# A pair's fourth step and its tail as one step of three rows, and last keys' transposes moved to VectorE, in a top-k attention with a low-rank mixer

## Chip, core and metric

One core of one Trainium2 chip runs the whole kernel. The metric is the device time in microseconds of one execution. The kernel before takes 1706.43 us (median of 3 runs, 1706.23 to 1707.57).

## The reference

Two blocks follow each other, all in float32 on 8 batches, 8 heads, 576 positions, head size 64:

```python
# attention, each batch and head
scores = q @ k.T / 8
kth = 32nd largest of each row of scores
attn = softmax(where(scores >= kth, scores, -1e9))   # sum + 1e-9 below
x = concat over heads of attn @ v                    # (8, 576, 512)
# mixer, each batch
u = x + (x.T @ U @ V).T                              # U 576x32, V 32x576
out = u + relu(u @ w_ch1) @ w_ch2                    # 512 -> 2048 -> 512
```

The mixer's parameters come in float64 and are turned into float32 on the chip.

## The kernel before

**Tiles.** Heads are worked in pairs; a batch has 4 pairs, the run 32 (g = 0 to 31, in the code NPAIR = 4, NP = 32). Of a head's 576 query rows 512 make four full tiles of 128 rows (t = 0 to 3); the last 64 rows of both heads of the pair share one tile, the *tail* (t = 4, NT). A full tile has two *lanes*, one for each head: 128 rows by 576 scores. The tail has one lane, with 64 rows of each head. `CH` = 5 tiles a pair, so 160 steps, one tile a step.

**What a tile goes through.** `scores` (L313): TensorE makes the products in the PSUM ring `sc` (two buffers of two banks), ScalarE copies them to `Ssb` (L351, tail L340). From pair 5 on (`blocked`) the top 32 are sought in a folded row: `fold` (L367) and `split` (L375) call `pair` (L380), in which POOL adds the two halves of the row as integers (L390), VectorE takes their maximum (L392) and POOL subtracts that from the sum (L393): `upper` holds the 288 larger ones of the pairs, `lower` the 288 smaller ones. `front` (L412) is a generator that the step loop advances piece by piece. On VectorE it takes the 16 largest of `lower` into the end of `upper` (L432, L434, L436: MAX8, MATCH_REPLACE8, MAX8), then four times the 8 largest of the 304 (L446 and L463), removing them in between (L458). Each of these lines loops over the tile's lanes, so a full tile alternates between its two rows, and each instruction of the tail follows the one whose result it needs. Then, one step later, comes what masks and weighs: ScalarE makes a *gap* row `E` (L488, a relu that is huge below the 32nd value), POOL subtracts it from the scores (L491), ScalarE takes the exponential with the row sum (L397). `E` is a ring of two buffers.

**Transposing the weights.** The values need the weights with keys on partitions. From pair 6 on (`shared`, `ROUNDED`) full tiles do this in two parts. `blocks` (L509): VectorE transposes the 32x32 blocks of each lane's first 512 keys into `y` (L518), four transfers on SP's queue write them to DRAM (`away`, L524), and `back` (L530) brings them back with ScalarE's queue as `PT` in the right place. The last 64 keys of both heads lie side by side in `Ssb` as one 128x128 block; this is transposed by TensorE in `turns` (L538, the transpose L557) and copied into `PT` by ScalarE (L558). Tails and earlier pairs are transposed wholly by TensorE (L552, L557, copies L553, L558). `values` (L567) multiplies: L587 with the block of last keys, L591 with the 512 keys of each head, and L577 in the tail; L600 copies the result into `XT`. `mixed` (L603) makes a pair's columns of u once its tail is through.

**MLP as filler.** The mixer's MLP of a batch is cut into single products by the generator `mlp` (L665: first layer L674 with the relu copy to `hT` L687, second layer L692), and the calls of `fill` (L762) drop as many products into TensorE's queue as a share says. So an MLP runs under the attention of the next batch, and the last MLP runs alone at the end. A step has 8 fills; a tail's step counts 0.65 of a full one (`SHORT`), and up to the middle of pair 8 the share is multiplied by 0.91 (`EARLY`):

```python
SLOTS, SHORT, EARLY = 8, 0.65, 0.91                    # L758
share = MLP_WORK / (NPAIR * SLOTS * (NT + SHORT))
due += share * (SHORT if t == NT else 1) * (EARLY if n <= 2 * ALONE + 2 else 1)
```

**Order.** The order of all engines' queues is written out by hand in the loop over n (L796): in step n `front` of tile n runs on VectorE, `scores` and `fold` of tile n + 1 are issued, masking and weights of tile n - 1 run, `blocks` of n - 1 is issued late in the step, `back` and `turns` of tile n - 2 follow, and `values` of tile n - 3. The first batch (n < 20, `ALONE`) has an order of its own, without filler.

Of the kernel before, what the change touches and what calls it, by code (L numbers as in the profile page):

```python
# [26 lines left out]
def kernel(  # L27
# [44 lines left out]
    ROUNDED = ALONE + 2 * CH  # L72
# [4 lines left out]
    HT = 10  # L77
# [235 lines left out]
    def scores(g, t):  # L313
# [4 lines left out]
        S2 = attn.tile([P, 2 * (S + TAIL)], F32, tag="Ssb", name="Ssb", bufs=4)  # L318
# [12 lines left out]
        if t == NT:  # L331
            sc = ps_s.tile([P, 2, 512], F32, tag="sc", name="sc")
            for i in range(2):
                for h in range(2):
                    lo = i * HALF + (TAIL if h and blocked(g) else 0)
                    hi = min(lo + HALF, S)
                    product(sc[half(h), i, 0 : hi - lo], h, lo, hi)
                    if hi - lo < HALF:
                        product(sc[half(h), i, hi - lo : HALF], h, 0, TAIL)
            nc.scalar.copy(S2[:, 0:S].rearrange("p (i n) -> p i n", i=2), sc[:, :, 0:HALF])  # L340
            if blocked(g):
                fronts_of[g, t] = sc[:, 0:1, 0:HALF]
            return
# [23 lines left out]
    def fold(g, t):  # L367

        if blocked(g) and g < NP:
            upper = attn.tile([P, 2, HALF + TOPK // 2], F32, tag="upper", name="upper")  # L370
            lower = attn.tile([P, 2, HALF], F32, tag="lower", name="lower", bufs=1)
            folds[g, t] = upper, lower
            pair(g, t, 0)
# [6 lines left out]
    def pair(g, t, stage):  # L380
# [10 lines left out]
        else:  # L391
            nc.vector.tensor_tensor(top, fronts_of.pop((g, t)), b, ALU.max)  # L392
# [19 lines left out]
    def front(g, t):  # L412
# [4 lines left out]
        if t == 0:  # L417
            dens[g] = small.tile([P, 2 * NT + 1], F32, tag="den", name="den", bufs=3)
        S2, den = S2s.pop((g, t)), dens[g]
        n = S2.shape[1]  # L420
        chunks = [S2[:, c] for c in range(n)]
        sums = [den[:, 2 * t + c : 2 * t + c + 1] for c in range(n)]
        first = small.tile([P, 2, 8], F32, tag="first", name="first", bufs=3)
        nmax = small.tile([P, 2], F32, tag="nmax", name="nmax", bufs=4)
        order = (1, 0) if n == 2 else (0,)
        folded = (g, t) in folds
        if folded:
            upper, lower = folds.pop((g, t))
            curs = [upper[:, c] for c in range(n)]
            spots = [[upper[:, c, HALF + i : HALF + i + 8] for c in range(n)] for i in (0, 8)]  # L430
            for c in order:
                nc.vector.max(spots[0][c], lower[:, c])  # L432
            for c in order:
                nc.vector.match_replace(lower[:, c], spots[0][c], lower[:, c], NEG)  # L434
            for c in order:
                nc.vector.max(spots[1][c], lower[:, c])  # L436
        else:
            curs = list(chunks)
            places = [
                attn.tile([P, 2, HALF + TOPK // 2], F32, tag="upper", name="upper")  # L440
                .rearrange("p c n -> p (c n)")[:, 0:S]
                for _ in range(n)
            ]
        ms = [first[:, c] for c in range(n)]
# [3 lines left out]
        early, pooled, gaps = ways(g, t)  # L448
        for i in range(1, TOPK // 8):
            if i == 1:  # L450
                nc.scalar.mul(nmax[:, 0:n], first[:, 0:n, 0], -SCALE)
                Es = {c: attn.tile([P, S], F32, tag="E", name="E") for c in early}
                for c in early:
                    weigh(chunks[c], Es[c], nmax[:, c : c + 1])
            for c in order:

                nxt = places[c] if i == 1 and not folded else curs[c]
                nc.vector.match_replace(nxt, ms[c], curs[c], NEG)  # L458
                curs[c] = nxt
            m8 = small.tile([P, 2, 8], F32, tag="m8", name="m8", bufs=4)  # L460
            ms = [m8[:, c] for c in range(n)]
            for c in order:
                nc.vector.max(ms[c], curs[c])  # L463
            yield
        for c in pooled:
            gap = attn.tile([P, S], F32, tag="E", name="E")
            nc.gpsimd.tensor_scalar(gap, chunks[c], ms[c][:, 7:8], NEG, ALU.is_lt, ALU.mult)
            nc.gpsimd.tensor_tensor(chunks[c], chunks[c], gap, ALU.add)  # L468
        for c in early:
            nc.vector.scalar_tensor_tensor(  # L470
                out=chunks[c],
                in0=chunks[c],
                scalar=ms[c][:, 7:8],
                in1=Es[c],
                op0=ALU.is_ge,
                op1=ALU.mult,
                accum_out=sums[c],
            )
        if t == NT:
            del qkTs[g]  # L480
        yield
        if gaps:
            lo, hi = min(gaps), max(gaps) + 1
            least = small.tile([P, 2], F32, tag="least", name="least", bufs=3)
            nc.scalar.mul(least[:, lo:hi], m8[:, lo:hi, 7], WIDEN)
            for c in gaps:
                gap = attn.tile([P, S], F32, tag="E", name="E")
                nc.scalar.activation(  # L488
                    gap, chunks[c], AF.Relu, bias=least[:, c : c + 1], scale=-WIDEN
                )  # L490
                nc.gpsimd.tensor_tensor(chunks[c], chunks[c], gap, ALU.subtract)  # L491
            yield
        ahead = order[0:1] if len(gaps) == 2 else ()
        for c in ahead:
            weigh(chunks[c], chunks[c], nmax[:, c : c + 1], sums[c])
            yield
        for c in order:
            if c not in early and c not in ahead:
                weigh(chunks[c], chunks[c], nmax[:, c : c + 1], sums[c])
# [4 lines left out]
    def shared(g, t):  # L504


        return t < NT and g * CH + t >= ROUNDED

    def blocks(g, t):  # L509


        E2 = probs[g, t]
        PT = attn.tile([P, 2 * NT + 1, P], F32, tag="PT", name="PT")
        PTs[g, t] = PT
        y = attn.tile([P, 4, 2, NT, BLK], F32, tag="y", name="y", bufs=1)
        for h in (1, 0):
            a = h * (S + TAIL)
            nc.vector.transpose(  # L518
                y[:, :, h].rearrange("p r c j -> p c r j"),
                E2[:, a : a + MAIN].rearrange("p (c r j) -> p c r j", c=NT, r=4),  # L520
            )
        away = dram.tile([P, 4, 2 * P], F32, tag="away", name="away")
        for a in range(4):
            nc.sync.dma_start(  # L524
                away[:, a].rearrange("(r i) n -> i r n", r=4),
                y[a * BLK : (a + 1) * BLK].rearrange("i r h c j -> i r (h c j)"),
# [3 lines left out]
    def back(g, t):  # L530

        if (g, t) in aways:
            nc.scalar.dma_start(
                PTs[g, t][:, 0 : 2 * NT].rearrange("p a n -> p (a n)"),
# [3 lines left out]
    def turns(g, t):  # L538


        E2 = probs.pop((g, t))
        nh = 2 if t < NT else 1
        if shared(g, t):
            PT = PTs[g, t]
        else:
            PT = attn.tile([P, 2 * NT + 1, P], F32, tag="PT", name="PT")
            PTs[g, t] = PT
        for h in range(0 if shared(g, t) else nh):
# [18 lines left out]
    def values(g, t):  # L567
# [4 lines left out]
        if t == NT:  # L572
# [13 lines left out]
            return  # L586
        nc.tensor.matmul(O, lhsT=vd, rhs=PT[:, 2 * NT], start=True, stop=False)  # L587
        PB = PT[:, 0 : 2 * NT].rearrange("p (a h) (c j) -> p h c a j", h=2, c=NT)
        for j in range(NT):
            for h in range(2):  # L590
# [3 lines left out]
                    rhs=PB[:, h, j] if shared(g, t) else PT[:, NT * h + j],  # L594
# [3 lines left out]
        if t == 0:  # L598
            XTs[g] = attn.tile([P, MAIN], F32, tag="XT", name="XT")
# [155 lines left out]
    STEPS = NP * CH  # L755


    SLOTS, SHORT, EARLY = 8, 0.65, 0.91  # L758
    share = MLP_WORK / (NPAIR * SLOTS * (NT + SHORT))
    fillers, mixing, due = [], [], 0.0  # L760

    def fill(k=1):  # L762
# [3 lines left out]
        for _ in range(k):  # L766
# [4 lines left out]
            due += share * (SHORT if t == NT else 1) * (EARLY if n <= 2 * ALONE + 2 else 1)  # L771
# [9 lines left out]

    def weighted(m):

        values(*divmod(m, CH))
        if m % CH == NT:
            mixing.append(mixed(m // CH, 5, 1 if m < STEPS - 1 else 0))
# [9 lines left out]
    for n in range(STEPS + 2):  # L796
        g, t = divmod(n, CH)
        if n < STEPS:
            if t == 0 and g + 1 < NP:
# [3 lines left out]
            fronts[n] = front(g, t)  # L803
            next(fronts[n])
        here, last = fronts.get(n, iter(())), fronts.pop(n - 1, iter(()))
        if n >= ALONE - 1 and n <= ALONE:

            if n < ALONE:
                next(last)
                values(*divmod(n - 3, CH))  # L810
# [3 lines left out]
                scores(*divmod(n + 1, CH))  # L814
                fold(*divmod(n + 1, CH))
                values(*divmod(n - 2, CH))
            list(turns(*divmod(n - 1, CH)))
            values(*divmod(n - 1, CH))
            if n < ALONE:
                split(*divmod(n + 1, CH))  # L820
# [8 lines left out]
            scores(*divmod(n + 1, CH))  # L829
            fold(*divmod(n + 1, CH))  # L830
# [8 lines left out]
            split(*divmod(n + 1, CH))  # L839
# [4 lines left out]
        ease = eased(*divmod(n - 1, CH))  # L844
        if n < ALONE:
            if ease:
                next(last, None)
            scores(*divmod(n + 1, CH))
            fold(*divmod(n + 1, CH))
            if n >= 3:  # L850
                values(*divmod(n - 3, CH))
# [12 lines left out]
            split(*divmod(n + 1, CH))  # L864
# [5 lines left out]
            if n >= 1:  # L870
                turning = turns(*divmod(n - 1, CH))
            continue
        away = n <= STEPS and shared(*divmod(n - 1, CH))
        if ease:
            next(last, None)
# [3 lines left out]
        if n + 1 < STEPS:  # L879
            scores(*divmod(n + 1, CH))  # L880
            fold(*divmod(n + 1, CH))
        next(turning, None)
        fill()
        next(turning, None)
        if n > ALONE and (n - 1) % CH < NT:
            next(last, None)
# [62 lines left out]
```

## Time and profile before

| what | value |
|---|---|
| median of runs | 1706.43 us |
| profiled execution | 1705.85 us |
| its span, first to last instruction | 1704.0 us |
| mean granted TensorE clock | 0.969 |
| busy PE | 1611.5 us, 95% |
| busy PEld (weight load) | 1218.9 us, 72% |
| busy DVE (VectorE) | 1484.2 us, 87% |
| busy ACT (ScalarE) | 1020.7 us, 60% |
| busy POOL (GpSimd) | 944.9 us, 55% |

The profile names engines PE (matmul), PEld (weight load), DVE, ACT, POOL, SP. Busy shares are averages over the first batch without filler (to about 192 us), the stretch of steps with filler (to about 1550 us) and the last MLP alone; so they are read by stage. A row of a timeline has start in us, duration in us, engine, line, operation, tiles written and read, shapes, count. An engine's instructions overlap a little, so costs are best taken from start to start. A row of waits has: engine, its tile and line, what ended the wait, total us, times, longest. An fp32 product is two matmul instructions; a transpose is one.

### The profile page before, as it was taken

The numbers are of one execution on the slowest core, as the hardware profiler recorded it, in microseconds if no ns is written. First come the engines' busy times: TensorE is split into PE (matmuls) and PEld (weight loads), VectorE is DVE, ScalarE is ACT, GpSimd is POOL, SyncE is SP. The second block draws the span as 40 slices with busy tenths as digits, with TensorE's granted clock in tenths as the row PEclk, the third lists the DMA queues.
The fourth block names the chain that finished last, engine by engine and source line by source line (L and its number), as shares of the span: only waits on it lengthen the run. The fifth ranks groups of instructions, "written<-read, shape, count | busy, mean of one in ns | idle before, by whom it ended". The sixth has DMA issues, their size and how long they took to land.

```text
span 1704.0 us, 29640 instructions
## 1 busy us (share of the span) xinstructions
PE 1611.5 (95%) x9489; PEld 1218.9 (72%) x9489; DVE 1484.2 (87%) x4317; ACT 1020.7 (60%) x2582; POOL 944.9 (55%) x749
## 2 busy tenths in 40 slices
PE   4567799999999999999999999999999999999999
PEld 2344566777777877788777877788777877788777
DVE  7999989999999999999999999999999999992000
ACT  4888797665656666565656666565655666563100
POOL 4778678666555565565555565565555565562000
PEclk7777899999999999999999999999999999999999
DMA  3323322344444444444444444444444444432010
GB/s 86 96 83 85 84 75 65 82 109 118 124 113 115 115 114 106 118 105 121 120 110 112 120 114 107 111 110 117 118 111 119 118 112 103 112 94 72 4 16 13
DMA packets 275837, 167.37 MB, mean 98 GB/s; under 512 B 173920, under 2 KB 260192, under 8 KB 275680
## 3 DMA queue, kind: packets, MB, share of 16 engines
q1 hardware_dynamic: 259648, 110.67, 27.7%
q10 hardware_dynamic: 16032, 54.79, 10.0%
q8 instruction: 75, 1.23, 0.3%
q14 instruction: 82, 0.67, 0.1%
HBM read 101.42 MB, written 63.96 MB: 97 GB/s over the span
## 4 chain that ended last, share of the span: by engine, by line
PE 79%; DVE 13%; ACT 3%; POOL 2%; DMA 2%; issue 1%; SPq 0%; DVEq 0%; POOLq 0%; ACTq 0%
PE mm L674 27%; PE mm L692 26%; PE sc L323 9%; PE O L591 6%; DVE upper L458 4%; DVE m L463 4%; PE O L577 2%; PE tp L557 2%; PE up L637 2%; DVE first L446 1%; PE O L587 1%; PE tp L552 1%; PE up L639 1%; PE pT L625 1%; DMA PT<-away 1%
## 5 line engine op out<-in xcount | busy, mean ns | idle before, releaser
L692 PE MATMUL mm<-hT,w 128*128 128x256 f32 (+1 forms) x2048 | 532.0, 408 | 0.0
L674 PE MATMUL mm<-uT,w 128*128 128x256 f32 (+1 forms) x2048 | 525.1, 408 | 0.0
L491 POOL TENSOR_TENSOR Ssb<-Ssb,E 128x576 f32<-128x576 f32 x271 | 378.9, 1416 | 239.5 <-ACT E L488 239.2
L674 PEld LDWEIGHTS mm<-uT,w 128*128 128x128 f32 x2048 | 380.1, 191 | 97.3 <-issue 2.9
L692 PEld LDWEIGHTS mm<-hT,w 128*128 128x128 f32 x2048 | 378.4, 192 | 93.2 <-issue 3.9
L463 DVE MAX8 m<-upper 128x8 f32<-128x304 f32 (+1 forms) x864 | 409.3, 512 | 3.6
L458 DVE MATCH_REPLACE8 upper<-m,upper 128x304 f32<-128x304 f32 (+1 forms) x576 | 286.8, 506 | 0.0
L390 POOL TENSOR_TENSOR lower<-Ssb 128x576 uint32<-128x576 uint32 (+1 forms) x135 | 174.0, 1289 | 152.1 <-ACT Ssb L351 57.8
L397 ACT ACTIVATE Ssb<-Ssb,nmax 128x576 f32<-128x576 f32 x286 | 221.5, 776 | 18.2 <-POOL Ssb L468 9.8
L393 POOL TENSOR_TENSOR lower<-lower,upper 128x576 uint32<-128x576 uint32 (+1 forms) x135 | 173.7, 1287 | 103.6 <-DVE upper L392 93.6
L323 PE MATMUL sc<-qkT 64*128 64x288 f32 x1334 | 211.4, 440 | 8.9 <-ACT Ssb L358 7.9
L687 ACT ACTIVATE hT<-mm 128x320 f32<-128x320 f32 (+1 forms) x256 | 104.9, 410 | 178.4 <-PE mm L674 172.5
L488 ACT ACTIVATE E<-Ssb,least 128x576 f32<-128x576 f32 x271 | 197.9, 769 | 5.2
L323 PEld LDWEIGHTS sc<-qkT 64*128 64x128 f32 x1334 | 115.8, 183 | 64.0 <-issue 22.5
L351 ACT COPY Ssb<-sc 128x576 f32<-128x576 f32 x216 | 127.6, 643 | 34.6 <-PE sc L323 33.0
L591 PE MATMUL O<-PT,va 128*64 128x128 f32 x2048 | 143.2, 283 | 3.3 <-DMA PT<-away 3.2
L518 DVE STREAM_TRANSPOSE y<-Ssb 128x512 f32<-128x512 f32 x208 | 135.6, 687 | 7.0 <-ACT Ssb L397 6.2
L704 DVE TENSOR_TENSOR oT<-uT,mm 128x320 f32<-128x320 f32 (+1 forms) x8 | 3.6, 455 | 142.4 <-PE mm L692 142.4
L591 PEld LDWEIGHTS O<-PT,va 128*64 128x64 f32 x2048 | 112.1, 139 | 19.9 <-DMA PT<-away 4.3
L432 DVE MAX8 upper<-lower 128x8 f32<-128x288 f32 x243 | 98.0, 440 | 19.6 <-POOL lower L393 18.4
L392 DVE TENSOR_TENSOR upper<-sc,Ssb 128x576 f32<-128x576 f32 (+1 forms) x135 | 92.5, 685 | 22.5 <-ACT Ssb L351 22.5
L458 DVE MATCH_REPLACE8 upper<-first,upper 128x304 f32<-128x304 f32 x243 | 110.2, 462 | 0.0
(91 smaller groups left out, 1881.1 us busy)
## 6 DMA issues: line engine op xcount, KB each, us to landing
away<-y SPq DMA_DIRECT2D x416, 128.0 KB, 2.4
PT<-away ACTq DMA_DIRECT2D x104, 512.0 KB, 3.3
raw<-in_moe_w_ch_dram SPq DMA_DIRECT2D x32, 512.0 KB, 3.9
va<-in_v_dram SPq DMA_DIRECT2D x64, 128.0 KB, 2.3
out_dram<-ob SPq DMA_DIRECT2D x57, 128.0 KB, 2.1
ld<-in_q_dram SPq DMA_DIRECT2D x108, 64.0 KB, 3.1
ld<-in_k_dram SPq DMA_DIRECT2D x108, 64.0 KB, 2.4
ld<-in_q_dram SPq DMA_DIRECT2D x108, 8.0 KB, 3.0
```

Of the source, the lines that this page charges most:

```text
L323: nc.tensor.matmul(out, lhsT=qkT[half(h), 0, cols(t)], rhs=qkT[half(h), 1, lo:hi], start=True, stop=True,)
L390: nc.gpsimd.tensor_tensor(bottom, a.bitcast(U32), b.bitcast(U32), ALU.add)
L393: nc.gpsimd.tensor_tensor(bottom, bottom, top.bitcast(U32), ALU.subtract)
L397: nc.scalar.activation(E, chunk, AF.Exp, bias=nmax, scale=SCALE, accum_out=total)
L458: nc.vector.match_replace(nxt, ms[c], curs[c], NEG)
L463: nc.vector.max(ms[c], curs[c])
L488: nc.scalar.activation(gap, chunks[c], AF.Relu, bias=least[:, c : c + 1], scale=-WIDEN)
L491: nc.gpsimd.tensor_tensor(chunks[c], chunks[c], gap, ALU.subtract)
L518: nc.vector.transpose(y[:, :, h].rearrange("p r c j -> p c r j"), E2[:, a : a + MAIN].rearrange("p (c r j) -> p c r j", c=NT, r=4),)
L591: nc.tensor.matmul(O[half(h)], lhsT=va[:, h, j, :], rhs=PB[:, h, j] if shared(g, t) else PT[:, NT * h + j], start=False, stop=(j == NT - 1),)
L674: nc.tensor.matmul(ph[:, 0:w], lhsT=w1[:, cc, f * P : (f + 1) * P], rhs=uT[:, cc, lo:hi], start=(cc == 0), stop=(cc == NC - 1),)
L692: nc.tensor.matmul(po[:, 0:w], lhsT=w2[:, f, c * P : (c + 1) * P], rhs=hTs[f][:, 0:w], start=(f == 0), stop=(f == NF - 1),)
```

## The change

From pair 4 on (the second batch) a list of steps takes the place of divmod: the steps of a pair are t = 0, 1, 2, and one step that holds tile 3 and the tail. `front` takes the tiles of a step and makes one list of lanes; the fused step has three, in the order head 1, head 0, tail, and every VectorE line loops over all three. The gaps of the three lanes are made one after another, then the subtractions and exponentials. A tail's scores are issued at the end of the step two before (t = 1), the fold of its row beside that of tile 3; the tail of pair 4 is folded too. The tail has tiles of its own with one buffer each (`Stail`, `tupper`, `tlower`, `PTt`). The values of the tail come ahead of those of tile 3 in the same step.

In the full tiles of pairs 6 to 31 the block of last keys goes the way of the others: a third VectorE transpose (128x128) in `blocks`, 288 in place of 256 columns in `y`, `away` and the transfers; `turns` returns at once for them, and L587 reads its block from the returned `PT`.

Fills stay 8 a step; the fused step counts 1.4 (`LONG`), and the share is divided by 3 + 1.4. The rings `hT` and `XT` shrink from 10 to 8 and from 2 to 1.

```diff
-    HT = 10
+    HT = 8
...
     def scores(g, t):
-        S2 = attn.tile([P, 2 * (S + TAIL)], F32, tag="Ssb", name="Ssb", bufs=4)
+        if t == NT and g >= NPAIR:
+            S2 = attn.tile([P, S], F32, tag="Stail", name="Stail", bufs=1)
+        else:
+            S2 = attn.tile([P, 2 * (S + TAIL)], F32, tag="Ssb", name="Ssb", bufs=4)
...
     def pair(g, t, stage):
-            nc.vector.tensor_tensor(top, fronts_of.pop((g, t)), b, ALU.max)
+            nc.vector.tensor_tensor(top, fronts_of.pop((g, t), a), b, ALU.max)
...
-    def front(g, t):
+    def front(tiles):
+        lanes = []
+        for g, t in tiles:
...
+            for c in (1, 0) if n == 2 else (0,):
+                slot = c if n == 2 or len(tiles) == 1 else 2
+                lanes.append((slot, S2[:, c], den[:, 2 * t + c : 2 * t + c + 1], ...
...
+        for at_, step in ((0, 0), (0, 1), (8, 0)):
+            for slot, upper, lower in halves:
+                spot = upper[:, HALF + at_ : HALF + at_ + 8]
+                if step:
+                    nc.vector.match_replace(lower, spot, lower, NEG)
+                else:
+                    nc.vector.max(spot, lower)
...
     def blocks(g, t):
-        y = attn.tile([P, 4, 2, NT, BLK], F32, tag="y", name="y", bufs=1)
-        for h in (1, 0):
-            a = h * (S + TAIL)
+        y = attn.tile([P, 4, 2 * NT + 1, BLK], F32, tag="y", name="y", bufs=1)
+        for i, a, c in ((1, S + TAIL, NT), (0, 0, NT), (2, MAIN, 1)):
             nc.vector.transpose(
-                y[:, :, h].rearrange("p r c j -> p c r j"),
-                E2[:, a : a + MAIN].rearrange("p (c r j) -> p c r j", c=NT, r=4),
+                y[:, :, i * NT : i * NT + c].rearrange("p r c j -> p c r j"),
+                E2[:, a : a + c * P].rearrange("p (c r j) -> p c r j", c=c, r=4),
             )
-        away = dram.tile([P, 4, 2 * P], F32, tag="away", name="away")
+        away = dram.tile([P, 4, (2 * NT + 1) * BLK], F32, tag="away", name="away")
...
     def turns(g, t):
+        if shared(g, t):
+            return
...
-            XTs[g] = attn.tile([P, MAIN], F32, tag="XT", name="XT")
+            XTs[g] = attn.tile([P, MAIN], F32, tag="XT", name="XT", bufs=1)
...
-    SLOTS, SHORT, EARLY = 8, 0.65, 0.91
-    share = MLP_WORK / (NPAIR * SLOTS * (NT + SHORT))
+    steps = [[(g, t)] for g in range(NPAIR) for t in range(CH)]
+    for g in range(NPAIR, NP):
+        steps += [[(g, t)] for t in range(NT - 1)] + [[(g, NT - 1), (g, NT)]]
+    SLOTS, LONG, EARLY = 8, 1.4, 0.91
+    share = MLP_WORK / (NPAIR * SLOTS * (NT - 1 + LONG))
...
     def weighted(m):
-        values(*divmod(m, CH))
+        for g, t in reversed(tiles(m)):
+            values(g, t)
...
         next(here, None)
-        fill(2)
+        fill()
+        if len(tiles(n + 2)) > 1:
+            scores(*tiles(n + 2)[1])
+        fill()
```

## The prediction

> **What bounds the kernel now.** First the page: where is which engine full?
>
> ```profile
> PE   4567799999999999999999999999999999999999
> DVE  7999989999999999999999999999999999992000
> PEclk7777899999999999999999999999999999999999
> ```
>
> Each digit is one slice of 42.6 us. From slice 10 on (429 us) TensorE is at 9 and stays there; VectorE is at 9 too, but stops in slice 37. The first batch (to 192 us) is VectorE's; the last three slices are the MLP of the last batch alone. What the change touches lies between. A table by stretch and the waits of 429 to 1390 us (five batches, 20 pairs of heads) tell the two engines apart:
>
> ```profile
> 621.00:813.00 192.00, 192.00 (x1160) 146.78 (x1160) 184.02 (x565) 117.62 (x304) 111.60 (x88) 1.00 0.45 114
> ```
>
> ```profile
> PE O L591 <- DMA PT<-away: 0.5, 1, 0.5
> ```
>
> ```profile
> DVE upper L392 <- ACT Ssb L351: 19.0, 19, 1.7
> DVE upper L432 <- POOL lower L393: 6.7, 10, 0.8
> DVE y L518 <- ACT Ssb L397: 4.5, 4, 1.1
> ```
>
> Columns of the first: stretch, length, busy PE, PEld, DVE, ACT, POOL. TensorE waits 0.5 us in 961; VectorE waits 30.2 us, 1.5 us a pair, nearly always once a pair. In the chain of waits the same piece (26 instructions of L674) begins at 637.21, 829.48 and 1021.75: 192.27 us a batch, 48.07 us a pair, TensorE's own. A busy TensorE is modelled, so I checked by starts: a 320-column product is two instructions 0.269 us apart, in the steady part and in the last MLP alone. There is no slack inside; an instruction taken from TensorE shortens the step.
>
> The Trainium skill ("Perfetto Trace Analysis", Identifying the Most-Contended Engine) says that matmul busy time is a bad measure and LDWEIGHTS busy a better one: here that is 146.78 of 192 us, 76%, which would leave VectorE (184.02) as the bound and the removal worth nothing, about 1706. The waits above decide against it.
>
> What is removed, on TensorE:
>
> ```profile
> 827.98 1.24 PE L323 MATMUL sc<-qkT 64*128 64x288 f32 x8
> 829.15 0.33 PE L557 MATMUL tp<-ident,Ssb 128*128 128x128 f32 x1
> 829.32 7.16 PE L674 MATMUL mm<-uT,w 128*128 128x320 f32 x26
> ```
>
> L557 is the transpose of a full tile's last keys: the next product starts 0.164 us (unrounded) after it. On VectorE, one row alone (the tail) against two rows in alternation (a full tile):
>
> ```profile
> 819.74 0.09 DVE L458 MATCH_VALUE_LOAD upper<-first,upper 128x8 f32 x1
> 819.82 0.46 DVE L458 MATCH_REPLACE8 upper<-first,upper 128x304 f32<-128x304 f32 x1
> 820.31 0.48 DVE L463 MAX8 m<-upper 128x8 f32<-128x304 f32 x1
> 820.83 0.09 DVE L458 MATCH_VALUE_LOAD upper<-m,upper 128x8 f32 x1
> ...
> 828.98 0.07 DVE L458 MATCH_VALUE_LOAD upper<-first,upper 128x8 f32 x1
> ...
> 829.86 0.84 DVE L463 MAX8 m<-upper 128x8 f32<-128x304 f32 x2
> 830.62 0.07 DVE L458 MATCH_VALUE_LOAD upper<-m,upper 128x8 f32 x1
> ```
>
> A round costs 1.09 us for one row alone and 1.64 us for two, 0.82 each: an instruction that needs its forerunner's result starts some 0.13 us later.
>
> **Part by part.** Sums are made against the profiled execution's 1705.85 us (span 1704.0 and 1.85 around it); the median shown is 0.58 more.
>
> *TensorE, removed.* Four L557 a pair in pairs 6 to 31: 104. At 0.164 us each 17.1 us. The nearest other row is L557 of the tail, after products, at 0.109 us, so 11.3 us if the difference comes back as a slower next load. I take 0.164: it is this instruction in this place. Their 104 copies on ScalarE (L558, 0.276 us) go too: 28.7 us off the path. The products read the same columns from a differently strided tile: L587's strided reading has its price in L591, which reads so already.
>
> *VectorE.* The tail's row alone takes 2.01 us (817.73 to 819.74) and three rounds of 1.09, 5.28 us. In a full step, first L432 to first L432 (845.77 to 855.59) is 9.82 us; less L392 0.65 and two transposes 1.21 leaves 7.96, 3.98 a row. Three rows should cost 3 times 3.98: 1.30 us less a pair. Added are four transposes of 128x128 a pair. Rows: 512 columns start 0.605 us apart, 1152 take 1.25; the line through them gives 0.28 for 128 (lower end a quarter of 0.605, 0.15; upper end 0.605 itself). So +1.12 a pair, from 0.60 to 2.42. In the stretch where VectorE sets the pace (the starts of L293 at 322.0, 368.1, 414.4, 460.4) a pair takes 46.15 us; it becomes 46.0, between 45.5 and 47.3. TensorE becomes 48.07 less 4 times 0.164, 47.41. VectorE stays below it over its whole range, by 1.4 us at my value: TensorE remains the bound and the removal counts in full.
>
> [...]
>
> *Fill.* A pair has 4 steps of 8 slots with weight 3 + 1.4 where it had 5 with 4 + 0.65. The share is divided by just that sum, so a pair still spends a quarter of an MLP, and the early 0.91 lasts to the same step (pair 8, t = 2). Zero. Where that 0.91 holds, VectorE paces: in pairs 6 and 7 the eight L557 become idle time, and VectorE's own 0.15 a pair is the gain, 0.3 us. So 96 of 104 count: 15.7 us.
>
> *Moved.* The tail's scores (PE), their copy (ACT L340), L390 and L393 on POOL and L392 on VectorE come earlier or behind the full tile's; numbers stay. On TensorE five groups of scores a pair remain; each change to 64 rows and back costs some 0.1 us as before. Zero; if the lone group pays both anew, 0.2 us times 28, 5.6 us. They stand two fills before the step's end, behind the L392 that frees their buffer; a step of 11 us leaves about 2 us.
>
> *SP and ACT queues.* Still 416 and 104 transfers, each 9/8 as large; landing 2.4 and 3.3 us becomes by ratio 2.7 and 3.7. Return issued 848.80, first use 857.61: 8.8 us of cover, so zero. The product with vd now waits for it too, 0.3 us sooner. Behind a late return stands all of TensorE's queue; uncovered it would cost up to 0.4 us a tile.
>
> *Ring sizes.* Eight hT tiles hold one half's 16 activations; the next half's first write follows TensorE's last reading of the old ones in its queue anyway. XT alone is read (L614) almost a step before it is written. Zero; without that cover a wait of a copy, 0.27 us a pair.
>
> *New wait.* A fused step has three gaps (L488) in an E ring of two.
>
> ```profile
> L491 POOL TENSOR_TENSOR Ssb<-Ssb,E 128x576 f32<-128x576 f32 x271 | 378.9, 1416 | 239.5 <-ACT E L488 239.2
> ...
> L488 ACT ACTIVATE E<-Ssb,least 128x576 f32<-128x576 f32 x271 | 197.9, 769 | 5.2
> ```
>
> The third gap waits for the first subtraction: 0.77 + 1.42 = 2.19 us against 1.54 after two gaps, 0.65 us idle, then 0.77. Queued behind it on ScalarE are hT's copy, XT's copy and the copies of the next scores. TensorE meanwhile has a fill, two value groups and the scores, over 3 us. Zero on the path; price in the rivals.
>
> *Pairs 4 and 5.* They take 52.0 and 50.6 us (L293), held by parameter work on POOL and waits for it. A folded tail and no lone row help VectorE; L390 and L393 of the tail (1.6 us) load POOL. TensorE idles 7.4 us from 192 to 288, which caps it. I take -1.5, between -5 and +3.
>
> *The end.* The last tile now needs the round trip through memory where a tail by TensorE stood. Gaps, subtractions and exponentials 5.7, transposes 1.5, transfers 6.4: 13.6 us, against 13 slots and small work of 14.7 us on TensorE. +1, between 0 and 4.
>
> Sum: -15.7 - 0.3 - 1.5 + 1 = -16.5, so 1689.3 and on the median's scale 1690. Its own range: low end 17.1 + 5 off, 1684; high end 10.5 off (96 times 0.109), +3 and +4 back, 1703, rarely above 1700.
>
> **Rivals.** *Slower, by the E ring.* If the 0.65 + 0.77 us reach TensorE through a late hT copy (two mm buffers, 2.15 us a group of four products), 28 pairs lose 1.42 us each, 39.8 us; less 16.5: 1730. It decides from 0.6 us a pair on (16.5/28). For it: half the fill is L674, whose copies are due every 2.15 us. Against it: ScalarE waits for TensorE's products now (hT L687 70.6 us in the five batches), not the other way. 11 in 100.
>
> *VectorE takes over.* Its demand nears 47.3 (dear transposes), or its waits of 1.5 us a pair remain beside 46.0 of work: 47.3 to 47.9 a pair against 48.07; 24 pairs give 4 to 18 us, and with the end (+4) and pairs 4 and 5 (+3) at their worst 1695 to 1709. For it: it is 96% full. Against it: its waits are those of the engine that is ahead, and they vanish when it is late. 9 in 100.
>
> *Only the dead time goes.* L557 counts 0.109: 1695, inside the forecast, which has 80 in 100.
>
> This kernel's measurement can tell about 0.2%, 3.4 us, from no change. The forecast lies wholly below 1703; the takeover splits into 3 faster, 4 same, 2 slower. Faster 0.83, same 0.04, slower 0.13. The range 1683 to 1704 leaves out the E ring, half the takeover and a few of the rest.
>
> **What would show it.** L557 down to 56 instructions; a batch of 190 us or a little less between repeats of the long L674 pieces; TensorE's waits still near nothing; VectorE's round with three rows 2.46 us; VectorE still waiting about 1 us a pair. Wrong: waits of mm L674 for ACT hT (the ring), or TensorE waiting for sc's buffers or PT with a VectorE that waits for nothing (takeover), or pairs 4 and 5 longer.

## The result: 5.2% slower, and the profile after

The changed kernel takes 1795.26 us (median), the kernel before 1706.86 us in the same session: ratio 1.052, 95% interval 1.0493 to 1.0547. The forecast was 1690, between 1683 and 1704. The profiled execution has a span of 1795.7 us at a mean clock of 0.952.

The page's slices, and the shares of the chain that ended last:

```profile
PE   4667889988898999989999999989999999999999
DVE  7999999989899988989989898989999898993000
PEclk7777999998999999999999999999999999999999
...
DVE 51%; PE 32%; DMA 5%; SPq 3%; issue 3%; ACT 2%; POOL 2%; ACTq 0%; DVEq 0%; POOLq 0%
```

Before, TensorE stood at 9 in every slice from the tenth on, and the chain had it at 79%. Now both engines have 8s in the middle and neither is full, as when a wait goes round between engines. By stretch (length, busy PE, PEld, DVE, ACT, POOL, clock):

```profile
621.00:813.00 192.00, 181.56 (x1061) 135.01 (x1060) 170.81 (x533) 103.53 (x257) 102.87 (x81) 0.97 0.45 114
```

In the same 192 us TensorE starts 1061 instructions where it started 1160, at a clock of 0.97 where it had 1.00. The waits of 429 to 1390 us that were not there before, of TensorE, VectorE and ScalarE:

```profile
PE mm L696 <- ACT hT L709: 39.4, 9, 5.2
```

```profile
DVE y L536 <- DMA away<-y: 48.2, 18, 3.8
```

```profile
ACT hT L709 <- DMA away<-y: 54.7, 9, 6.7
```

(Lines shift: the MLP's first layer is L696, its copy L709, the transposes into `y` L536, `away` L542, the return L551, the search's VectorE lines L458 and L463 are L475 and L480.) All three hang on the transfer from `y` to `away`, TensorE through ScalarE's copy. VectorE's wait comes 18 times in 18.7 pairs, once a pair; the other two rows have 9 times each. The transfer is late because of SP's queue, which issues it. One such place, SP first (SPq and ACTq are the queues in which SP and ScalarE issue transfers):

```profile
968.96 1.76 SPq L542 DMA_DIRECT2D away<-y  x4
970.76 0.65 SPq L247 DMA_DIRECT2D ld<-in_q_dram  x1
...
984.57 0.64 SPq L280 DMA_DIRECT2D vt<-in_v_dram  x1
...
986.53 8.48 SPq L542 DMA_DIRECT2D away<-y  x8
```

The 21 loads of the next pair stand here one after another, 970.76 to 985.2, 14.4 us: some 0.69 us each to issue. Now VectorE, ScalarE and TensorE:

```profile
977.46 1.48 DVE L536 STREAM_TRANSPOSE y<-Ssb 128x512 f32<-128x512 f32 x3
...
990.73 0.71 DVE L536 STREAM_TRANSPOSE y<-Ssb 128x512 f32<-128x512 f32 x1 [3.10 <-DMA away<-y]
```

```profile
990.67 0.33 ACTq L551 DMA_DIRECT2D PT<-away  x1
991.04 0.39 ACT L709 ACTIVATE hT<-mm 128x256 f32<-128x256 f32 x1 [6.14 <-DMA away<-y]
```

```profile
968.58 1.89 PE L696 MATMUL mm<-uT,w 128*128 128x256 f32 x8
...
991.48 3.78 PE L696 MATMUL mm<-uT,w 128*128 128x256 f32 x8 [4.59 <-ACT hT L709]
```

`y` was full at 978.9; its transfer is issued at 986.5, 7.7 us late, behind the loads and two stores of the output (985.31 to 986.44). The return on ScalarE's queue waits for it to land, holds ScalarE 6.14 us with the copy of hT behind it, and that copy holds TensorE 4.59 us. The next tile's transposes wait 3.10 us for the one `y` buffer.

Behind the wait the products are slow as well. Eight of L696 take 3.78 us there and 1.89 at 968.58: the granted clock is 0.50 from 991 to 996. In the five stretches of some 192 us from 429 to 1390 its mean is 0.94, 0.97, 0.97, 0.99 and 0.98, and 1.00 in each of them before. A batch of four pairs takes 205.6 us where it took 192.27, so these 18.7 pairs lose 62 us; the shortfall of the clock makes up to some 29 of them. That is an estimate from the means, and an upper one, for VectorE sets the pace in part of this time; no run took this apart from the waits.

Before, the loads did the same, but in a step without any `away`, because the tile before it was a tail:

```profile
826.06 1.76 SPq L524 DMA_DIRECT2D away<-y  x4
827.87 0.64 SPq L247 DMA_DIRECT2D ld<-in_q_dram  x1
...
842.64 0.64 SPq L280 DMA_DIRECT2D vt<-in_v_dram  x1
844.63 12.82 SPq L524 DMA_DIRECT2D away<-y  x8
```

The next `y` was written from 843.31 to 844.52, when the last load had just been issued at 843.3. The cover was complete and had 1.2 us over. Fusing the tail's step took it away.

### The profile page after: what moved, and what is told of

The parts are those of the page before. It is cut to its first block, busy times and chain, and to the rows that moved or that the text cites. A ratio compares the mean times of both kernels' runs of the same rounds, so it can differ in the third digit from the quotient of the medians.

```text
span 1795.7 us, 29193 instructions
## 1 busy us (share of the span) xinstructions
PE 1640.0 (91%) x9385; PEld 1224.4 (68%) x9385; DVE 1499.8 (84%) x4426; ACT 988.6 (55%) x2422; POOL 949.6 (53%) x751
## 4 chain that ended last, share of the span: by engine, by line
DVE 51%; PE 32%; DMA 5%; SPq 3%; issue 3%; ACT 2%; POOL 2%; ACTq 0%; DVEq 0%; POOLq 0%
DVE upper L475 15%; DVE m L480 13%; PE mm L696 13%; PE mm L714 10%; DVE upper L450 6%; DVE first L462 5%; DVE y L536 4%; DMA away<-y 4%; DVE lower L448 3%; PE sc L326 3%; DVE upper L397 3%; PE O L613 2%; SPq L542 2%; DMA ld<-in_q_dram 1%; PE O L597 1%
## 5 line engine op out<-in xcount | busy, mean ns | idle before, releaser
L696 PE MATMUL mm<-uT,w 128*128 128x256 f32 (+1 forms) x2048 | 550.2, 420 | 52.6 <-ACT hT L709 52.4
L696 PEld LDWEIGHTS mm<-uT,w 128*128 128x128 f32 x2048 | 387.9, 195 | 169.7 <-ACT hT L709 62.3
L510 POOL TENSOR_TENSOR Ssb<-Ssb,E 128x576 f32<-128x576 f32 x243 | 339.9, 1418 | 289.8 <-ACT E L509 289.5
L480 DVE MAX8 m<-upper 128x8 f32<-128x304 f32 (+1 forms) x864 | 398.8, 507 | 0.7
L475 DVE MATCH_REPLACE8 upper<-m,upper 128x304 f32<-128x304 f32 (+1 forms) x576 | 284.5, 502 | 0.0
L709 ACT ACTIVATE hT<-mm 128x320 f32<-128x320 f32 (+1 forms) x256 | 104.4, 408 | 250.1 <-PE mm L696 174.5
L395 POOL TENSOR_TENSOR lower<-Ssb 128x576 uint32<-128x576 uint32 x108 | 154.1, 1427 | 161.4 <-issue 74.7
L536 DVE STREAM_TRANSPOSE y<-Ssb 128x512 f32<-128x512 f32 (+1 forms) x312 | 157.4, 549 | 90.8 <-DMA away<-y 71.7
L402 ACT ACTIVATE Ssb<-Ssb,nmax 128x576 f32<-128x576 f32 x258 | 200.9, 780 | 51.6 <-DMA away<-y 37.8
L326 PE MATMUL sc<-qkT 64*128 64x288 f32 (+1 forms) x1334 | 218.4, 452 | 10.8 <-ACT Ssb L359 7.7
L450 DVE MAX8 upper<-lower 128x8 f32<-128x288 f32 x488 | 194.0, 442 | 18.0 <-POOL lower L398 17.7
L509 ACT ACTIVATE E<-Ssb,least 128x576 f32<-128x576 f32 x243 | 176.2, 768 | 4.3
L326 PEld LDWEIGHTS sc<-qkT 64*128 64x128 f32 (+1 forms) x1334 | 119.3, 188 | 81.1 <-issue 39.4
L475 DVE MATCH_REPLACE8 upper<-first,upper 128x304 f32<-128x304 f32 x244 | 110.1, 460 | 0.0
L622 ACT COPY XT<-O 128x128 f32<-128x128 f32 x128 | 34.1, 266 | 131.1 <-PE O L613 131.0
```

The source lines that it names most:

```text
L326: nc.tensor.matmul(out, lhsT=qkT[half(h), 0, cols(t)], rhs=qkT[half(h), 1, lo:hi], start=True, stop=True,)
L402: nc.scalar.activation(E, chunk, AF.Exp, bias=nmax, scale=SCALE, accum_out=total)
L450: nc.vector.max(spot, lower)
L509: nc.scalar.activation(gap, chunk, AF.Relu, bias=least[:, c : c + 1], scale=-WIDEN)
L510: nc.gpsimd.tensor_tensor(chunk, chunk, gap, ALU.subtract)
L536: nc.vector.transpose(y[:, :, i * NT : i * NT + c].rearrange("p r c j -> p c r j"), E2[:, a : a + c * P].rearrange("p (c r j) -> p c r j", ...
```

## The experiments

Each is compared with the kernel before on the same chip (1706.6 to 1706.7 us).

### The loads apart (after_spread)

`load` of blocked pairs becomes a generator with a yield after each transfer:

```diff
-            if t == 0 and g + 1 < NP:
+            if t == 0 and g + 1 <= NPAIR + 1:
                 load(g + 1)
...
                 blocks(*tile_)
+        if n < STEPS and t == 2 and g + 2 < NP:
+            loading = parts_of(g + 2)
+        for _ in range(7 if t != 1 else 0):
+            next(loading, None)
```

> The changed kernel with a pair's 21 loads taken apart: from pair 6 on, seven of them behind the away transfers of each of the three steps t = 2, fused and t = 0, in place of all 21 at the start of t = 0. Theory SP (the 21 loads hold SP's queue for some 14.5 us, in a step that now has away transfers of its own, so these start 7 to 8 us late): all of the loss goes and the forecast's sum shows, 1686 to 1696 us; no wait of y or of ScalarE for away. Theory RING (three rows a step, the third gap's wait and late hT copies cost it): stays at 1780 to 1800. Theory BYTES (transfers 9/8 as large collide): stays at 1780 to 1800.

1703.6 us, ratio 0.9983 (0.9973 to 0.9992). All of the loss is gone, 91.7 us, and both other theories with it. The table of 621 to 813 us:

```profile
621.00:813.00 192.00, 192.00 (x1155) 146.20 (x1155) 187.14 (x583) 113.86 (x280) 112.67 (x89) 1.00 0.49 125
```

TensorE is full again at a clock of 1.00, while the DMA share (the last column but one) rose from 0.45 to 0.49: the engines that move the data had room, and what was short was the queue that issues. The edit moves the loads behind the `away` transfers as well as apart; which of the two does more was not tried. But 1703.6 is not 1690, and lies above the expectation's 1686 to 1696; the rest of this section is half about that.

### The cover taken from the kernel before (before_collide)

```diff
-            if t == 0 and g + 1 < NP:
+            if t == (0 if g < NPAIR + 2 else 2) and g + 1 < NP:
                 load(g + 1)
-            if t == 1 and g + 1 < NP:
+            if t == (1 if g < NPAIR + 2 else 3) and g + 1 < NP:
                 ready = prep(g + 1)
```

> The kernel before with one thing moved: from pair 6 on the loads are issued at the start of step t = 2 in place of t = 0, behind one tile's away transfers and ahead of the next one's, and the qkT transpose two steps later. No fused step, no larger transfers. Theory SP: a loss of the changed kernel's size, 2 to 4 us a pair over 26 pairs, 1760 to 1800 us, with VectorE waiting at y for away and ScalarE behind its return transfers. Theories RING and BYTES: 1705 to 1710.

1769.1 us, ratio 1.0362 (1.0344 to 1.0379). Two steps' shift of 21 issues, and of the transpose of `qkT` that reads what they load, brings 62 us and the same waits, VectorE's and ScalarE's of 429 to 1390 us:

```profile
DVE y L518 <- DMA away<-y: 46.6, 19, 3.3
```

```profile
ACT hT L687 <- DMA away<-y: 41.2, 10, 7.2
```

It is the place of the loads in SP's queue that costs, with or without three rows and larger transfers. Why 62 us and not 88 was not followed up.

### Two y buffers (after_y2)

```diff
-        y = attn.tile([P, 4, 2 * NT + 1, BLK], F32, tag="y", name="y", bufs=1)
+        y = attn.tile([P, 4, 2 * NT + 1, BLK], F32, tag="y", name="y", bufs=2)
...
-        raw = mlpp.tile([P, 2 * C], U32, tag="raw", name="raw", bufs=3)
+        raw = mlpp.tile([P, 2 * C], U32, tag="raw", name="raw", bufs=2)
```

> The changed kernel with two y buffers in place of one (and, for space, two raw buffers in place of three, which only the parameters use up to pair 8). Theory SP: VectorE's wait at y for away goes, but the return transfer still stands in ScalarE's queue and waits for the late away, so hT's copies and TensorE stay late: part of the loss is left, 1720 to 1785 us. If VectorE's wait alone made the loss: 1686 to 1700. Theory RING or BYTES: 1780 to 1800.

1805.8 us, ratio 1.058 (1.0564 to 1.0596), above all that was expected (1720 to 1785 by theory SP): nothing got better. VectorE's wait only changed its name, now for the exponential that stands behind the return in ScalarE's queue:

```profile
DVE y L536 <- ACT Ssb L402: 67.4, 19, 5.2
```

ScalarE's copy of `hT` still waits 55.7 us for `away` (9 times, before this edit 54.7), and TensorE 40.4 us for that copy. The wait for the buffer is a symptom; ScalarE's queue passes the delay on. Over four batches of the steady part one takes 204.6 us against 205.6; the 10 us more come early, where pair 5 takes 57.1 us and took 49.7, with one raw buffer less (that cause was not tried by itself).

### Last keys alone (before_keys)

The edits of `blocks`, `back`, `turns` and `values` that the change's diff shows, in the kernel before, with its 160 steps.

> The kernel before with the second half of the change alone: last keys of full tiles by VectorE, transfers 9/8 as large, no L557 for them; steps as before, so the step with the loads has no away transfers. Theory SP: faster by TensorE's removed transposes, 1688 to 1694 us. Theory RING: the same. Theory BYTES: slower than 1706, up to 1790.

1713.95 us, ratio 1.0045 (1.003 to 1.006). Theories SP and RING missed: the kernel is slower, though 104 of L557's transposes are gone. Theory BYTES (slower than 1706, up to 1790) has it at its lower end. Where VectorE sets the pace (pairs 6 to 9, 46.8, 49.0, 46.8 and 48.0 us against 46.0, 46.3, 46.0 and 46.9) TensorE meets the return late:

```profile
399.74 0.76 PE L588 MATMUL O<-PT,vd 128*128 128x128 f32 x2 [3.07 <-DMA PT<-away]
```

At this place it is not the cover that is short: the last load was issued at 367.1, and the `away` transfers go out from 390.6 on, when `y` has just been filled. The third transpose, the larger transfers and the first product of the values, which now needs the return as well, all stand in this path; what each costs was not separated. From 322 to 520 us such waits are 3.4 us more than before, at the end (1390 to 1600 us) 3.1: 6.5 of the 8.9 us between the two profiled runs. Where the rest lies was not settled. But in the steady part, too, a batch takes 192.12 us against 192.27, where 2.6 us less were forecast. That is the second error.

### What a transpose costs TensorE (before_tp2, before_tpmoved, fused_spread)

The starts in the trace show where the time went. Before, the last product of the scores is followed by L557 after 0.333 us, that by the MLP's product after 0.164, and this takes 0.270. Without L557, after_spread and before_keys have 0.332, and then 0.373 for that first product (of 320 columns), 0.103 more than L557 left it. Three kernels to test it:

```diff
 # before_tp2
         nc.tensor.transpose(tp, E2[:, a : a + P], ident)
+        if shared(g, t):
+            nc.tensor.transpose(tp, E2[:, a : a + P], ident)
 # before_tpmoved
-        next(turning, None)
+        if not shared(*divmod(n - 2, CH)):
+            next(turning, None)
         fill()
         next(turning, None)
 # fused_spread: after_spread with blocks, back, turns and values of the kernel before
```

> The kernel before with L557 of full tiles issued twice, into the same tile with the same result: 104 transposes more, each behind a transpose and not behind the scores. Theory SWITCH: 0.109 us each on TensorE, 1.74 us a batch; over the 96 where TensorE sets the pace 10.5 us: 1717. Theory FULL (a transpose costs 0.164 wherever it stands): 2.6 us a batch, 1722.

1716.1 us, ratio 1.006 (1.0048 to 1.0073); a batch 194.02 us, 1.75 more: 0.109 a transpose. As SWITCH said.

> The kernel before with L557 of full tiles moved behind the next fill, so that it stands between products and a product follows the scores. Theory SWITCH: the product behind the scores takes 0.373 in place of 0.270, L557 0.109 in place of 0.164, the net 0.048 more a tile: 0.77 us a batch, 4.6 in all, 1711. Theory FULL: L557 costs 0.055 less and nothing else changes, 1701.

1711.9 us, ratio 1.0031 (1.0019 to 1.0044); a batch 193.01, 0.74 more. Scores, product, and L557 between products:

```profile
823.26 1.24 PE L323 MATMUL sc<-qkT 64*128 64x288 f32 x8
824.43 0.81 PE L674 MATMUL mm<-uT,w 128*128 128x320 f32 x2
825.08 0.38 PE L737 MATMUL tp<-ident,oT 128*128 128x128 f32 x2
825.29 0.27 PE L557 MATMUL tp<-ident,Ssb 128*128 128x128 f32 x1
825.40 3.94 PE L674 MATMUL mm<-uT,w 128*128 128x320 f32 x14
```

824.43 to 825.08 is 0.65 for two instructions that take 0.54 elsewhere; L557 takes 0.11. The same transposes in another place make the kernel slower.

> after_spread with the second half of the change undone: three-row steps and spread loads, but the last keys of full tiles by TensorE (L557's transpose and its copy) as before. Theory SWITCH (behind the scores whoever comes next pays some 0.103 us for the change of shape; L557 paid it, and without it the first product does, so removing L557 saves 0.164 - 0.103 = 0.06 us): 96 times 0.06 more than after_spread, 1709 us, a batch 1.0 us longer. Theory FULL (the removal is worth 0.164 and something else took it back): 1719.

1709.6 us, ratio 1.0023 (1.0014 to 1.0031): 6.0 us above after_spread, a batch 192.46 against 191.24. So the last keys on VectorE are worth 6.0 us where SP's queue has room, and the three-row steps, with the loads apart, cost 3.0 us.

### The three-row step in pair 4 (spread_yplaces, spread_gap3, spread_both, after_gap3)

after_spread still has waits of TensorE at 248 and 255 us. ScalarE and POOL there:

```profile
247.85 1.44 ACT L519 ACTIVATE E<-Ssb,least 128x576 f32<-128x576 f32 x2
253.82 0.78 ACT L519 ACTIVATE E<-Stail,least 128x576 f32<-128x576 f32 x1 [4.53 <-POOL Ssb L520]
```

```profile
249.79 1.28 POOL L187 TENSOR_TENSOR w<-w,raw 128x512 uint32<-128x512 uint32 x1
251.15 1.28 POOL L189 TENSOR_TENSOR w<-w,raw 128x512 uint32<-128x512 uint32 x1
252.39 2.77 POOL L520 TENSOR_TENSOR Ssb<-Ssb,E 128x576 f32<-128x576 f32 x2
```

The third gap waits for the E ring, the first subtraction waits behind parameter work on POOL, and XT's copy behind the gap keeps TensorE 4.3 us:

```profile
255.77 1.12 PE L582 MATMUL tp<-ident,Ssb 128*128 128x128 f32 x4 [4.28 <-ACT XT L632]
```

```diff
 # gap3: the third gap in a buffer that is free at that moment
+                if c == 2:
+                    gap = attn.tile([P, NT + 1, P], F32, tag="PTt", name="PTt", bufs=1)
+                    gap = gap.rearrange("p c n -> p (c n)")[:, 0:S]
+                else:
+                    gap = attn.tile([P, S], F32, tag="E", name="E")
 # yplaces: the unfolded rows' working copies (pair 4's fused step alone)
+                if len(tiles) > 1:
+                    if not places:
+                        wide = attn.tile([P, 4, 2 * NT + 1, BLK], F32, tag="y", name="y", bufs=1)
...
+                    places[slot] = wide[:, slot * S : (slot + 1) * S]
...
-        bound = tiles(n + 1)[:1] == [(NPAIR + 1, 0)]
+        bound = False
```

> after_spread with one thing more: in the one fused step whose full rows are not folded (pair 4) the working copies of the two rows lie in the y buffer, which is free until pair 6, in place of both upper buffers, so the next tile's fold need not wait for the end of the step. In after_spread TensorE waits 2.3 us for a score buffer and 4.3 us for a copy between 245 and 256 us, and 10 us at half the clock follow. Expected: those waits go, 3 to 5 us of 1703.6 off: 1699 to 1701. If they only move to the next step: 1703 to 1705.

1703.6 us, ratio 0.9984 (0.9976 to 0.9993): no gain. The wait for a score buffer is gone and the one for XT's copy is 6.5 us in place of 4.3: handed on.

> after_spread with the third gap in the PTt buffer. In the steps from pair 5 on ScalarE waited 0.86 us for the ring and TensorE for nothing, so nothing there; in pair 4, where POOL is busy with parameters, the third gap waited 4.5 us and XT's copy and a transpose behind it kept TensorE 4.3 us. Theory RING ONCE: 2 to 4 us of 1703.6 off, 1700 to 1702. If the wait is only handed on: 1703 to 1704.

1700.1 us, ratio 0.9961 (0.9949 to 0.9974): 3.5 us better, the fastest kernel of the study. The ring did reach TensorE, once.

> after_spread with both edits for pair 4: working copies of the unfolded rows in the y buffer and the third gap in PTt. TensorE's two waits of pair 4, 2.3 and 4.3 us, and the half clock behind them should go: 1698 to 1701. If they are handed on: 1703 to 1704.

1700.35 us, ratio 0.9964 (0.9951 to 0.9976): the same as spread_gap3; the working copies are worth nothing.

> The changed kernel with a place of its own for the third gap (the tail's PTt buffer, free at that moment), so that it need not wait for the first subtraction in the E ring. Theory SP: the ring is not what the change lost; the loads still hold SP's queue: 1786 to 1797 us, the wait of the third gap gone. Theory RING: below 1740.

1789.7 us, ratio 1.0494 (1.0478 to 1.051): 5.6 us of the 88, and the interval overlaps that of the changed kernel (1.0493 to 1.0547). The third gap no longer waits, and the waits for `away` are still there (ScalarE's copy of `hT` 76.3 us in the whole run, 74.0 without the edit).

## Where the prediction went wrong

**The step that failed is the one on SP and ACT queues.** It said "Still 416 and 104 transfers", took the return's cover of 8.8 us from a place after the loads, and came to zero. It counted what the change adds to the queue and not what stands beside it: the 21 loads, 14.4 us, at the head of the step t = 0, which had no `away` only because the tile before was a tail. With the loads apart the kernel gains 91.7 us. No rival held this; the main one on the slow side, the E ring, was a wrong place for the loss, and what it cost is 3.5 to 5.6 us in all. The sign that was named for the ring, the first layer's products waiting for ScalarE's hT, did appear (39.4 us): it shows that ScalarE is late, and not what holds ScalarE.

**The removal was sized 0.164 us a transpose and is worth 0.06.** Forecast 15.7 us, measured 6.0 (fused_spread to after_spread). The low end of the prediction, 0.109, was not low enough: not only the difference came back "as a slower next load", but the whole change of shape, 0.103 us. The trace of before had a row for it: behind the 32-column products of L625 the first MLP product takes 0.346 us where 0.245 is the mean.

**Pairs 4 and 5 and the end.** Forecast were -1.5 and +1, and -0.3 for pairs 6 and 7, in sum -0.8; the three-row steps without the last keys' part measure +3.0, of which the E ring in pair 4 is 3.5. The end by itself fits: in after_spread 108.3 us lie between the last transpose of qkT and the last MLP's first product, before 106.6: +1.7, within 0 to 4.

Together 91.7, some 10 and some 4 us are the 105 between 1690 and 1795. The kernels of this section were built one from the other, so the differences must add up; that each has the cause named rests on the rows above.

**What held.** TensorE is the bound where the queues run: 104 transposes more, 0.109 us each in the steady part, made the kernel 9.5 us longer. A round of three rows costs what was worked out, 2.46 us, in the changed kernel's chain of waits:

```profile
959.48 1.33 DVE upper L475 x3
960.81 1.13 DVE m L480 x3
```

The 128x128 transposes start 0.193 us before the next instruction, inside the 0.15 to 0.605 given. The 0.28 taken was a slip: the line through 0.605 for 512 columns and 1.25 for 1152 gives 0.22 for 128. With the loads apart VectorE did not take over, the fill was neutral (a batch of fused_spread takes 192.46 us, before 192.27), and no row shows a wait for the smaller rings.

The Trainium skill ("DMA: Bandwidth & Descriptors", Issuing engines are not separate DMA queues) says that the time a sequencer takes to issue is usually small beside the transfer. Here a load takes 0.69 us to issue and lands in 1.9 to 3.3 us, so that its issue is 0.2 to 0.4 of the transfer; but 21 issues in one queue add up to 14.4 us, and that sum is what the kernel met.

## What to carry to other kernels

Before a step is removed, list what every queue does during it, the queues that only issue transfers too: an idle queue in a step that looks empty may be the room in which a long run of issues fits, and one run of 21 issues delays everything that stands behind it in order. Price a removed instruction by the starts of the instruction after it, in a place of the trace where the pair that will become neighbours already stands side by side. And a wait that disappears when a buffer is added may only have moved to the next engine in the ring, as two `y` buffers showed.

## What the runs showed of the hardware that was not expected

**A change from 64-row products to 128-row ones costs the next instruction 0.055 or 0.103 us, by what it is**, and 0.097 before it: 0.333 from a full tile's last score product to whatever comes next, where score products follow each other by 0.236. The Trainium skill ("TensorEngine Tiling (Array Packing)", Key Properties) says that changing the tiling mode drains TensorE; the rows agree, and show here that the price falls on both sides of the change and is less when a transpose follows.

**VectorE's maximum with both inputs in SBUF waits for POOL's.** In the changed kernel the tail's maximum reads a copy in SBUF where the full tiles' reads the score buffer. In after_spread, VectorE, then POOL, at two places:

```profile
755.76 1.16 DVE L407 TENSOR_TENSOR upper<-Stail 128x288 f32<-128x288 f32 x1
...
899.81 0.53 DVE L407 TENSOR_TENSOR upper<-Stail 128x288 f32<-128x288 f32 x1
```

```profile
755.18 1.42 POOL L405 TENSOR_TENSOR lower<-Ssb 128x576 uint32<-128x576 uint32 x1 [1.86 <-issue]
756.56 1.02 POOL L405 TENSOR_TENSOR lower<-Stail 128x288 uint32<-128x288 uint32 x1
...
898.60 1.42 POOL L405 TENSOR_TENSOR lower<-Ssb 128x576 uint32<-128x576 uint32 x1 [2.29 <-DVE upper L485]
899.98 1.01 POOL L405 TENSOR_TENSOR lower<-Stail 128x288 uint32<-128x288 uint32 x1
```

It ends 0.32 us after POOL's instruction has ended (756.60 and 756.92; 900.02 and 900.34), however early it began: median 1.16 us against 0.447 in the kernel before, where one input lay in PSUM. Six of those overlapped a POOL instruction of L390 and took 0.441 to 0.450 us all the same. The prediction moved this instruction with the words "numbers stay"; it costs some 0.5 us a pair, and VectorE had the slack. The Trainium skill ("SBUF — State Buffer", SBUF: two separate sides) describes an exclusive lock of a shared port pair, which a VectorE instruction with two SBUF inputs and a GpSimd instruction that reads SBUF take in turn, and the rows agree. No run was made to separate this from other causes.
